# A written-out instruction order exchanged for another one, with one output store moved to a second queue

## Chip, cores and metric

The kernel runs on one core of one Trainium2 chip, as one launch. The metric is the device time of the launch in microseconds (us); shorter is better. Before the change it took 362.02 us (median of 3 runs, 361.42 to 363.49).

## What is computed

The inputs go through a linear attention with a decaying state, then a gated two-layer block. With batch B=4, heads H=8, sequence S=768, head size D=48, and x of width 384 made of the heads' outputs:

```python
for t in range(S):                                   # attention
    cur = einsum('bhd,bhe->bhde', u * k_t, v_t)
    y[:, :, t] = einsum('bhd,bhde->bhe', r_t, state + cur)
    state = w_t[..., None] * state + einsum('bhd,bhe->bhde', k_t, v_t)
h = gelu(x @ w_in)                                   # 384 -> 1024, tanh form
u, v = h[..., :512], h[..., 512:]
v_n = (v - mean(v)) / sqrt(var(v) + 1e-6) * g_ln
v_s = einsum('ts,bsd->btd', w_sg, v_n) + b_sg        # over the sequence
out = x + (u * v_s) @ w_out                          # 512 -> 384
```

## The kernel before, in words

The recurrence is done in 24 chunks of 128 time steps, six to a batch. A chunk's decays are running products over time (`decays`, lines 562 to 585, VectorE scans), its keys and receptances are scaled by them, and the rest of a chunk is small matmuls. The gated block works per batch on 128 rows for v (`v_piece`, L954) and on halves of 384 columns for u, the gate and the output (`u_piece`, `gate_piece`, `out_piece`). Each product of it is three matmuls with the operands split in a high and a low part (L950, L951, L952). The last batch's gate uses sums of halves of the matrices instead (`first_sum`, `second_sum`, `third_sum`). Checks of the inputs' range (`range_check`, `f64_check`) run on ScalarE from data loaded for that alone, and end in one flag (`verdict`, L1260) on which the program branches at its end (L1431, L1433).

Nothing is scheduled at run time. Every unit of work is a generator that yields steps, and the string `ORDER` (L40) says in which order the steps are taken and on which engine each one runs: 1785 words such as `p14S`. The first letter is the kind of work, the number its index (chunk or piece), the last letter the engine: P TensorE, D VectorE, A ScalarE, G GpSimd, S SyncE. `run` (L252) goes through the words and `step` (L259) emits each one's instructions, so the words of one engine, from left to right, are that engine's program. Each engine takes its own instructions strictly in this order and waits at one until its inputs, and the buffer that it takes, are there.

Kinds that are spoken of: r, o, q, p are the loads of a chunk's decays, keys and receptances, values, and token-major keys (`load_w` L528, `load_kr` L535, `load_v` L544, `load_rk` L552); w `own_weights` (L622); e `decayed_k`; f `decays`; t `move` (L912), three pairs of small DMAs that put a chunk's outputs in place; C `split_x` (L924), which waits for them; i `f64_check`, y `range_check`, g `early_sums`, n `late_sums`, each a load and then work on it; K `v_piece`, J `u_piece`, m `gate_piece`, u `out_piece`, M `verdict`. A word of J, m or u on TensorE is three matmuls.

E is `stretch` (L819), one word on TensorE for chunks 6 to 23. It takes together the last products of chunk n, products of chunk n+1 and scores of chunk n+2. Between its first group of matmuls (`pe_own`, L701) and a later group that uses the array's rows in another way, `behind` (L664) puts an instruction of SyncE:

```python
fence = nc.sync.nop()                                   # L667
tc.add_manual_dep(fence.ins, first.ins.name, sync, reason="row tiles")
tc.add_manual_dep(then.ins, fence.ins.name, sync, reason="row tiles")
```

SyncE waits there for the first group and TensorE's later group waits for SyncE. There are 18 of these marks, one in each stretch. SyncE also issues every DMA of the kernel, so a DMA whose word stands behind an E word is issued after that stretch has begun, however early its buffer is free.

TensorE's results go to four accumulators of one bank each (`m_ps`, three of them, and `resets` after chunk 7), which ScalarE or VectorE must empty before TensorE can use them again.

Of the kernel before, what the change touches and what calls it, by code (L numbers as in the profile page):

```python
# [45 lines left out]
c0S o4S p4S t1S t1S t1S q3S q5S v2P z3P f4D s3D e4G k4D f4D h0A w4D h0D w4D j3A C0A K0P K0P F2A F2A H3A j4A d3A K0P
K0A K0G p5S r5S C1A j5A C1G a4A k3P H4P k3A x3P w4D D3D f4D f5D H4A q4S h1S t2S t2S o5S t2S v3P D3D f5D f5D k5P w5G
w5G w5D K1P v3A v3P x4P w4A K1P K1P h5S h4S h3S d4A f4G D4D f5D D4D e5G z4P o7S r6S o6S p6S p7S F3A F3D h1A C2A f5D
h1D k5A f5G s4D K1A K1D C2D h4A h4D H5P H5A a5A h3A h3D h5A h5D k4P k4D v4P x5P K2P J1P K2P K2P d5G v4A v4P K1A K1D
K1G K0A K0G D5D w5A f6D f6D F4A F4A z5P K1G K0G w6D w6G K0G J3P J3P J1P s5D f6D e6D K1A K1A K1D w7D v5P v5A J1P J1A  # L50
# [10 lines left out]
u0P w10G m7D f11D f11D r12S p13S o12S e11G t6S t6S t6S I10A m7A s10D m7D w11D w11A D9D D9D u0D w13G w13G m6P m6P m6P
m5P m6P m6D m6D f12D d10A r13S m6A m6D e12D f12D C6G C6D p12S m5P m5P m5P E9P w12D m5P m4P m4P m4P K6P K6P f13D I11A
C7A C7D F9A w12G D10D D10D F9D s11D o13S q11S u0S q12S f12D f12D K6P C8A K6A K6D K6A C8G r14S m5P m5D w12D f13D e13D
w12D w13D K7P m4P K7P K7P K7A K7D E10P K8P f13D f13D d11A F10A K6D K6G w13G I12A K7A F10A D11D s12D m5D m5A f14D m4P
# [2 lines left out]
t7S t7S t7S o15S q13S r15S C9A C9G s13D K8A K6D K8D w15D D12D w14D u3P u3P J9P J9P K8A K8D K8G C10A u5D w15D r16S u4S
J9P J9A w14A u5S K9P K9P K9P u3P K8D K8D f15D C10D K8A K8D K9A C11A K9G K9A C11G J8P E12P s14D J8P J8P K9G K9G K9G u3P
f16D u3D p16S p17S u3S o17S f15D f15D K11P w15A I14A K11P K11P K11A K11D d13G K9A K9G a16A K11A J8A F12D D13D D13D K9D
f15D F12A e15D K10P K10P K10P K10A K10G J13P J13P m9P w16D w16G a15G w16D f16D J13P J13A m10P m10P m10P E13P m11P m11P  # L70
# [5 lines left out]
m13P m13P o18S C12A C12G d16A E15P w19D D16D w19D w19D f19D C13A C13G a19G D16D o19S J15P J15P J15P J15A m12P m12P
m12P m14P m13P s17D f18D f19D e18D f19D f19D m13D m13D w18A I17A F15A F15A q18S p20S r20S d17A C14A e19G w20G C14G
w20G m12P m12P m15P m15P m12D m12D m13A m13D m12A m12D E16P f20D D17D f20D s18D w20D F16A F16D r21S o20S m14P m14P
m15P m15P m15P K12P K12P K12P K12A K13P m15P K13P K13P K12D e20D I18A K12A K12D f20D m14P m14P m14P m14D w19A K13A
E17P K12G a20G K13G f21D f20D K13A K13D m14D s19D w20A F17D F17D f21D K12G K12G a21G K12G D18D D18D I19A K13G K13D  # L80
# [5 lines left out]
J23P J23P J19P J23P J21P K17P J19A J21P J21P J21A I21A K17P K17P K17A K17D J23A J17P J17P F19A J17P J17A i6S i6A K17A
K17D K17G K17G m16P w23D w23D f23D f23D f23D K17A K17A K17D q22S p22S o22S q21S m18P J22P f22D D20D m17P m17P m17P
m17P m18P m16P m16P m16P m16P J22P J22P m18P m18P m17P m18P m16P m16D m16D m16A e22G d21A m17P m17D m18P m16D w23A
J22A E20P w22G w22G a22G w22D w22D m18D m18D D21D D21D m19P I22D m17D s22D m18A F20A F20A m17A m18D m17D m19P m19P
# [275 lines left out]
def rwkv_gmlp(ctx: ExitStack, tc: tile.TileContext, wpad, kr, vtok, ktok, vt, u, ucol, w_in, consts_, w_sgT, w_out, out):  # L365
    nc = tc.nc
# [1244 lines left out]
```

## Time and profile before

| | before |
|---|---|
| median of 3 runs | 362.02 us (361.42 to 363.49) |
| the profiled execution | 365.26 us |
| its span, first to last instruction | 363.5 us |
| mean granted TensorE clock | 0.986 |
| busy: TensorE, VectorE, ScalarE, GpSimd | 343.0, 273.3, 222.1, 139.2 us |
| DMA: packets' share of the 16 engines' span | 49.9% |

The span is what the trace covers; 1.8 us of the profiled execution lie outside it. Busy time of an engine is the time in which it had an instruction of its own running; waits, branches and DMA issues are not counted. Every number of the trace comes from that one execution.

### The profile page before, as it was taken

What the parts mean: (1) busy time and instruction counts of PE and PEld (TensorE: products, weight loads), DVE (VectorE), ACT (ScalarE), POOL (GpSimd) and SP (SyncE); (2) the same over time, 40 slices, a digit from 0 to 9 for tenths busy, and PEclk for the clock granted to TensorE, in tenths of its full rate; (3) what the DMA queues carried; (4) which work ended last, traced back from release to release, by engine and by line L of the source; (5) the groups of instructions that cost most, each with busy time, mean ns of one, the idle gap of its engine ahead of it and who ended that gap; (6) DMA issues with size and microseconds to landing.
All of it is one profiled execution on the core that took longest, in us unless ns stands there. A gap on an engine that the chain in (4) does not pass through costs nothing.

```text
span 363.5 us, 11014 instructions
## 1 busy us (share of the span) xinstructions
PE 343.0 (94%) x4447; PEld 314.9 (87%) x4447; DVE 273.3 (75%) x537; ACT 222.1 (61%) x598; POOL 139.2 (38%) x222
## 2 busy tenths in 40 slices
PE   7997999999999996999999998999979869999995
PEld 6785788899999895899999897889977869999994
DVE  7998899998998839867779795756734234777684
ACT  1776997886445535862626663483443397898782
POOL 8283641217343223365415233633021836126500
PEclk9899999999999998999999999999999989999999
DMA  7978994512385274424266117431254765534542
GB/s 261 350 266 274 310 338 146 201 59 91 128 261 173 71 245 122 166 89 140 64 206 189 45 34 261 133 130 60 70 153 146 246 213 180 156 128 125 182 151 91
DMA packets 28470, 60.46 MB, mean 166 GB/s; under 512 B 3456, under 2 KB 13184, under 8 KB 28416
## 3 DMA queue, kind: packets, MB, share of 16 engines
q1 hardware_dynamic: 28416, 59.73, 49.9%
q8 instruction: 36, 0.59, 0.6%
q14 instruction: 18, 0.15, 0.1%
HBM read 53.82 MB, written 4.72 MB: 161 GB/s over the span
## 4 chain that ended last, share of the span: by engine, by line
PE 73%; DMA 8%; POOL 5%; ACT 5%; DVE 4%; issue 3%; SPq 1%; POOLq 0%; DVEq 0%
PE m_ps L950 14%; PE m_ps L952 13%; PE m_ps L951 13%; PE resets L950 4%; PE a_ps L678 4%; PE resets L951 4%; PE resets L952 4%; PE y_ps L701 3%; PE y_ps L712 2%; DMA vtok<-in_w_sgT 2%; DMA KR<-in_wpad 2%; DMA RK<-in_ktok 2%; DMA x<-y 1%; PE y_ps L685 1%; PE m_ps L481 1%
## 5 line engine op out<-in xcount | busy, mean ns | idle before, releaser
L950 PE MATMUL m_ps<-wsgh,vn 128*128 128x384 f32 x114 | 39.6, 347 | 2.0 <-DVE o L1256 2.0
L653 ACT ACTIVATE a<-KR,own 128x64 f32<-128x64 f32 x152 | 38.3, 337 | 5.1 <-DVE own L647 4.1
L952 PE MATMUL m_ps<-wsgh,vn 128*128 128x384 f32 x114 | 38.7, 340 | 0.0
L951 PE MATMUL m_ps<-wsgl,vn 128*128 128x384 f32 x114 | 38.7, 340 | 0.0
L950 PE MATMUL m_ps<-xT,winh 128*128 128x384 f32 x87 | 30.8, 354 | 3.2 <-DVE o L1256 2.9
L952 PE MATMUL m_ps<-xT,winl 128*128 128x384 f32 x87 | 29.7, 341 | 0.0
L951 PE MATMUL m_ps<-xT,winh 128*128 128x384 f32 x87 | 29.7, 341 | 0.0
L617 POOL TENSOR_TENSOR KR<-KR,W 128x512 f32<-128x512 f32 x14 | 16.7, 1190 | 23.5 <-DVE KR L585 13.0
L987 POOL TENSOR_TENSOR st<-st,mhalf 128x1 f32<-128x1 f32 x24 | 13.8, 575 | 29.1 <-DVE st L985 13.4
L950 PEld LDWEIGHTS m_ps<-wsgh,vn 128*128 128x128 f32 x114 | 21.9, 192 | 3.1 <-DVE o L1256 2.3
L950 PE MATMUL m_ps<-g,wouth 128*128 128x384 f32 x72 | 24.3, 337 | 0.0
L952 PE MATMUL m_ps<-g,woutl 128*128 128x384 f32 x72 | 24.2, 336 | 0.0
L951 PE MATMUL m_ps<-g,wouth 128*128 128x384 f32 x72 | 24.2, 336 | 0.0
L678 PE MATMUL a_ps<-KR 64*64 64x128 f32 (+1 forms) x768 | 22.8, 256 | 0.0
L1016 ACT ACTIVATE u<-m_ps 128x384 f32<-128x384 f32 x29 | 14.1, 487 | 13.3 <-PE m_ps L952 13.2
L951 PEld LDWEIGHTS m_ps<-wsgl,vn 128*128 128x128 f32 x114 | 21.9, 192 | 0.3
L701 PE MATMUL y_ps<-a,vtok 64*64 64x64 f32 x768 | 21.4, 224 | 0.8 <-ACT a L979 0.8
L701 PEld LDWEIGHTS y_ps<-a,vtok 64*64 64x64 f32 x768 | 16.2, 134 | 6.6 <-issue 2.5
L952 PEld LDWEIGHTS m_ps<-wsgh,vn 128*128 128x128 f32 x114 | 21.7, 191 | 0.0
L950 PE MATMUL m_ps<-winh,xT 128*128 128x512 f32 x45 | 18.6, 414 | 3.2 <-DVE g L1052 3.2
L372 ACT COPY x<-y_ps 128x384 f32<-128x384 f32 x20 | 9.6, 478 | 19.3 <-PE y_ps L701 7.3
L568 DVE TENSOR_TENSOR_SCAN W<-W,D 128x516 f32<-128x516 f32 x16 | 21.0, 1315 | 0.2 <-DMA W<-in_wpad 0.2
(372 smaller groups left out, 1085.7 us busy)
## 6 DMA issues: line engine op xcount, KB each, us to landing
KR<-in_kr SPq DMA_DIRECT2D x24, 512.0 KB, 4.9
RK<-in_ktok SPq DMA_DIRECT2D x20, 384.0 KB, 4.2
W<-in_wpad SPq DMA_DIRECT2D x24, 258.5 KB, 3.3
KR<-in_wpad SPq DMA_DIRECT2D x9, 517.0 KB, 3.8
vtok<-in_vtok SPq DMA_DIRECT2D x24, 192.0 KB, 4.5
out<-o SPq DMA_DIRECT2D x21, 192.0 KB, 3.0
vn<-in_w_in SPq DMA_DIRECT2D x6, 512.0 KB, 6.1
KR<-in_w_in SPq DMA_DIRECT2D x6, 512.0 KB, 4.1
```

The source lines that it names most:

```text
L372: nc.scalar.copy(o, i) if e == "ACT" else engine[e].tensor_copy(o, i)
L568: nc.vector.tensor_tensor_scan(Suf[:, WL - 1:0:-1], W[:, WL - 1:0:-1], r_one if early else D1[:, WL - 1:0:-1], 0.0, ALU.mult, ALU.add)
L617: engine[op.e].tensor_tensor(cols(x.K), cols(x.K), blocks(x.Suf, 2), ALU.mult)
L653: nc.scalar.activation(a[:, j, p], eyes, AF.Copy, scale=o[:, j, p:p + 1])
L678: nc.tensor.matmul(ps_[64 * c_:64 * c_ + 64, j, p * C:p * C + (2 * T if c_ < turn else T)], x.K[rows, at:at + T], r_, start=True, stop=True)
L701: m = nc.tensor.matmul(place(y, j, q, r, c_), x.V[64 * c_:64 * c_ + 64, h * D - up(p, j):h * D - up(p, j) + 64], x.a.tile[64 * c_:64 * c_ ...
L712: m = behind(m, nc.tensor.matmul(place(y, j, q, r, c_), S2.tile[64 * j:64 * j + 64, 16 + 64 * p - up(p, j):80 + 64 * p - up(p, j)], x.R[64 ...
L950: nc.tensor.matmul(ps, lh, rh, start=(i == 0), stop=False)
L951: nc.tensor.matmul(ps, lh, rl, start=False, stop=False)
L952: nc.tensor.matmul(ps, ll, rh, start=False, stop=(i == n - 1))
L987: nc.gpsimd.tensor_tensor(rstd, var, c.mhalf, ALU.pow)
L1016: nc.scalar.activation(h_.u[f].tile, ps, AF.Gelu_apprx_tanh)
```

## The change

The 1785 steps are the same, with the same arithmetic, and `ORDER` takes them in another order. 207 of them run on another engine: 59 go from GpSimd to VectorE and 58 the other way, 26 each way between GpSimd and ScalarE, 20 from ScalarE to VectorE and 17 back, one from SyncE to ScalarE. The 515 TensorE words are the same 515 in another order. An output store of the last batch may now name ScalarE, whose own DMA queue it then uses; one word does, `u23A`, the last half of the last piece. The rest of the file is unchanged.

The diff, cut to the stretches that are spoken of below:

```diff
 ORDER = """
-r0S o0S b0S r1S w0G w0P w0A f0D f0D f0D f0D f0D e0G f0G f1D f1D f1D k1S k1D f1D k1D o1S H0P z0P w0A w1D w1P j1A k1D
...
-m4D J11P J11P J11P J11A K8P E11P m4D m4A m5D m4D F11A F11A p15S u2S p14S o14S J10P J10P J10P J10A u4P I13A q14S a13G
-K7G K7G w14G w14D K7G f14D K6D u5P u5P u5P u5P u4P u4P u4P K8P K7D w15D e14D f14D f14G K7A D12D u4D K7D K6A K6A a14G
...
-K13D q19S J18P J18P J18P J18A u11P E18P u11P I20A o21S u8S t9S r23S p23S t9S t9S q20S o23S u11P u10P u11P u9P u9P J19P
...
-m19P J20P J20P J20P J20A m19P m19P m19D m19D m19A E21P I23D d22G i1S i1A g0S g0S g0G g0G m19D g0D g0D y1S t10S t10S
-t10S y1S q23S C18A C18G D22D D22D y1A y1A u12P u13P u13P u13P u12P u14P u14P u13P m20P m20P u13D u13S s23D m20P m20P
...
-C19D g1S g1S g1D g1G g1G F22A F22D D23D K18P K18P K18P K18A K18G C20G C20G K18A K18D K18G K18G K18G K18G g1G K18G K18G
-E23P m22P m22P F23D F23D m21P m22P m22P m21P y4S y4A y4A u14S i8S y2S y2S i8A m22D m22D m22A m22D K20P m23P i5S i5A
...
-y11A M0D M0D M0D M0D u22P u23P u21P u23P u22P u21P u21P u23P u23D u23S M0D u23D u23S M0D u21P u21D u21S u22P u22P
-M0D u22D u22S M0P M0D
+r0S o0S w0G f0D f0D f0D f0D f0D e0D r1S b0S f0G f1D k1S k1D k1D w0P w0A w0A a1A j1A o1S q0S k2S r2S H0P z0P w1G w1P
...
+D8D D8D w10A a10G u0D m7P m7P m7P m4P p11S o11S f11D f11D f11D f11D m7P m7P m7P m7D E8P F8A m4P F8D w11D w11D p12S u1S
+r12S q10S u2P u2P w11D u2D e11G d9G m4P w12G w12G m4P m4P m4P m5P m5P m5P m5P m6P m5P m6P I10A q11S t6S t6S t6S m7D
...
+w12A a13G C8G C8G w13D K6G w13D f13D f13D K7P E10P J11P K7P d11G K6A K7A K7G K7A J11P J11P J8P J8P K8P K8P K8P J11A
+F10D F10D D11D s12D m5D m5D K6G K6G K6G e13G f14D K7D q15S p14S o14S I12A E11P J8P r15S o15S K6A K6A K6D m5A m5D K7G
+K7G K8A w13D w13D f14D F11A F11A a14A J8A I13A K8G K8A t7S t7S q13S t7S J9P u5P J9P J10P J10P J10P J10A J9P w14D f14D
...
+o18S f18D u8P u8P u8P u8D w20D E15P D16D f18D D16D f18D r19S t8S t8S q17S t8S u8S o19S u6P f18D u6D u7P u7P C12A C12D
...
+w19G w19D w19A f20D K13P K13P K13P E17P f21D K13A K13D m13D F17A F17D s19D o21S p21S e20G f20D t9S q21S t9S t9S K13A
...
+m16P e22D f22G m18P m16P m16P m18P m17P m16P m16D m16D m16A d21A m16D w23G w23G m17P m17D m17D m17A m19P E20P f23D
+F20A F20A w22D w22G D21D D21D I22A w23D w23G J20P J20P J20P J20A m19P s22D m19P m19D m17D m19D u11S i8S i8A t10S t10S
+t10S C18A C18G J21P J21P m18P m18P m18P J21P J21A m19A m18P m18D m18D m18A m18D i5S i5A d22G C19G C19D u12P u12P E21P
+m19D u14P u14P u14P g1S g1S g1G g1G i9S i9A q23S I23D u12P u12P u12D u12S i2S i2A u13P u13P u13P u13P m22P m22P g1D
...
+K19G K19G E23P F23A F23A i1S i7S t11S t11S t11S m21P y3A y3A m23P m23P m23P m23D m23D m23A m21P m21P m21P m21D m21D
...
+u23P u22P u21P u22P u19S u18D u18S u23P u21P u21P u22P u23P u21P u21D u21S u22P u22D u22S u23P u23D u23S u23D u23A M0D
+M0D M0D M0D M0D M0D M0D M0P M0D
 """
...
     def dma(kb, **kw):
-        return Op({"SP": 0.62 if kb in (16, 48) else 0.47}, kb=kb, **kw)
+        return Op(kw.pop("on", {"SP": 0.62 if kb in (16, 48) else 0.47}), kb=kb, **kw)
...
-            yield dma(192 // parts, free=[o], apart=k < parts - 1)
-            nc.sync.dma_start(out[b, ms, half * HALF + k * w:half * HALF + (k + 1) * w], o.tile[:, 0:w])
+            op = yield dma(192 // parts, free=[o], apart=k < parts - 1, **({"on": {"SP": 0.47, "ACT": 0.47}} if b == B - 1 else {}))
+            (nc.scalar if op.e == "ACT" else nc.sync).dma_start(out[b, ms, half * HALF + k * w:half * HALF + (k + 1) * w], o.tile[:, 0:w])
```

## Rows read from the trace of the kernel before

**Rows 1.** The page's busy times, share of the span and instructions of each engine.
```profile
PE 343.0 (94%) x4447; PEld 314.9 (87%) x4447; DVE 273.3 (75%) x537; ACT 222.1 (61%) x598; POOL 139.2 (38%) x222
```

**Rows 2.** Waits of TensorE: for whom; us in total, times, longest.
```profile
PE m_ps L950 <- DVE o L1256: 4.9, 2, 2.9
PE m_ps L950 <- DVE g L1052: 3.2, 1, 3.2
...
PE resets L950 <- ACT xT L372: 0.9, 1, 0.9
PE y_ps L701 <- ACT a L979: 0.8, 1, 0.8
...
PE resets L952 <- POOL xT L945: 0.4, 1, 0.4
```

**Rows 3.** Windows: length; busy PE, PEld, DVE, ACT, POOL; PEclk; DMA share, GB/s.
```profile
0.00:10.00 10.00, 7.54 (x40) 7.07 (x41) 7.60 (x15) 2.58 (x7) 8.75 (x35) 0.92 0.79 261
...
70.00:80.00 10.00, 10.00 (x113) 9.10 (x112) 9.96 (x25) 8.32 (x23) 1.55 (x4) 1.00 0.09 30
...
140.00:150.00 10.00, 9.17 (x139) 8.31 (x140) 9.96 (x20) 6.79 (x22) 4.00 (x6) 0.83 0.34 105
...
290.00:300.00 10.00, 6.82 (x25) 5.71 (x24) 3.11 (x6) 9.46 (x23) 3.81 (x8) 0.83 0.63 211
```

**Rows 4.** Waits of SyncE's queue: the 18 marks of the stretches.
```profile
SPq L667 <- PE y_ps L701: 89.3, 18, 9.3
```

**Rows 5.** Timeline of SyncE, 100 to 145 us: start, us, then the issue.
```profile
120.40 0.33 SPq L533 DMA_DIRECT2D W<-in_wpad  x1
128.43 0.33 SPq L556 DMA_DIRECT2D RK<-in_ktok  x1
...
129.29 0.42 SPq L556 DMA_DIRECT2D RK<-in_ktok  x1
```

**Rows 6.** Timeline of TensorE, 126 to 148 us.
```profile
127.77 0.46 PE L701 MATMUL y_ps<-a,vtok 64*64 64x64 f32 x16
...
130.20 0.44 PE L950 MATMUL m_ps<-xT,winh 128*128 128x384 f32 x1
...
131.35 0.34 PE L950 MATMUL m_ps<-xT,winh 128*128 128x384 f32 x1
...
131.87 0.34 PE L950 MATMUL m_ps<-g,wouth 128*128 128x384 f32 x1
...
140.83 0.44 PE L950 MATMUL m_ps<-xT,winh 128*128 128x384 f32 x1 [2.90 <-DVE o L1256]
```

**Rows 7.** The chain that ended last, in order of time: start, us, what.
```profile
129.29 5.96 DMA RK<-in_ktok
...
219.80 5.05 DMA x<-y
...
261.34 6.55 DMA vtok<-in_w_sgT
...
282.67 6.16 DMA KR<-in_wpad
```

**Rows 8.** Timeline of VectorE, 0 to 20 us: one line of the kernel twice.
```profile
8.91 1.19 DVE L1303 TENSOR_SCALAR vn<-vn 128x512 int32<-128x512 int32 x1
...
13.50 0.41 DVE L1303 TENSOR_SCALAR vn<-vn 128x512 int32<-128x512 int32 x1
```

**Rows 9.** Timeline of all engines from 345 us to the end: the flag's steps.
```profile
356.51 0.17 DVE L1263 TENSOR_SCALAR chk<-chk 128x12 f32<-128x12 f32 x1
...
356.71 0.17 DVE L1265 TENSOR_REDUCE cnt<-chk 128x1 f32<-128x12 f32 x1
...
358.82 0.15 DVE L1275 TENSOR_TENSOR cnt<-cnt 128x1 f32<-128x1 f32 x1
...
359.12 0.19 PE L1278 MATMUL m_ps<-cnt,ones 128*1 128x1 f32 x2
...
359.70 0.14 DVE L1280 TENSOR_SCALAR bad<-m_ps 1x1 int32<-1x1 f32 x1
```

More of the change, by code (lines that the diff above doesn't have):

```diff
@@ L46 @@
[L46 to L50, printed above, removed]
@@ L61 @@
[L61 to L64, printed above, removed]
-m4D J11P J11P J11P J11A K8P E11P m4D m4A m5D m4D F11A F11A p15S u2S p14S o14S J10P J10P J10P J10A u4P I13A q14S a13G
@@ L66 @@
-K7G K7G w14G w14D K7G f14D K6D u5P u5P u5P u5P u4P u4P u4P K8P K7D w15D e14D f14D f14G K7A D12D u4D K7D K6A K6A a14G
[L67 to L70, printed above, removed]
@@ L76 @@
[L76 to L80, printed above, removed]
@@ L86 @@
[L86 to L89, printed above, removed]
-m19P J20P J20P J20P J20A m19P m19P m19D m19D m19A E21P I23D d22G i1S i1A g0S g0S g0G g0G m19D g0D g0D y1S t10S t10S
@@ new lines @@
+w1A H0A w1A f1D f1D f1D k1D k1D k1P s0D f1D e1G k2D f1D k2D k0S k0D k2D k0D v0P H1P z1P s1D k0D x0P k2D k0D f2D f2D
+f2D o3S j2A j0A v0A D0A D0D H1A v0P F0A a2A F0A k1A o2S q3S k0P k0A d1A w2G w2P w2A w2A w3G e2G f2D f2D r3S f2G f3D
+f3D f3D k4S q1S k4D v1P v1A x1P D1D f3D D1D f3D e3G k4D k4D k3S k3D q2S o4S t0S t0S t0S k2P k2A H2P a3A H2A d2A j4A
+v1P z2P w3P F1A F1A C0A k4D k4P k3D f3G h2S h2A h2G s2D w3D r4S x2P f4D k5S c0S D2D D2D f4D w3A f4D f4D v2P v2A p4S
+C0P d3A z3P v2P e4G C0A s3D k5D k3D F2A F2A k4A k5D h0S t1S t1S t1S p5S k3D w4D k5D r5S C1A C1D w4D w5D H3P H3A h0A
@@ new lines @@
+j3A h0G j5A a4A K0P K0P K0P K0A H4P v3P v3A x3P w5G D3D w4D H4A w4A h1S q4S o5S h1A k3P f5D f4D D3D t2S h5S t2S t2S
+K1P K1P v3P x4P f5D k5D K0D d4D f4D e5G D4D D4D f5D a5A k3A C2A C2D h1D F3A h5A F3A k5P h5D k5A h3S h3A h3G K0A K0G
+K1P K1A o6S h4S h4A q5S z4P q6S p6S J1P H5P J1P H5A J1P f5D s4D v4P v4A f5D w5D w5A r6S t3S k6S o8S t3S t3S J2P J2P
+J2P x5P v4P K1D K1A h4D d5D f5D D5D z5P f6D s5D f6D K0G w6G J0P J0P J0P K1G F4A F4A v5P J2A K0G K0A K1G K2P e6D J0A
+k6D w6D k6D K1D k6D v5A v5P K0A C3A C3D j6A k6D K0D k6D k8S k8D o7S r7S F5A F5A t4S t4S t4S p8S k6D k8D J1A K1A K1A
@@ new lines @@
+K1D k8D f7D H6P H6A t5S t5S t5S C4A C4G K2P K2P j8A K2A K2D k8D e7D k8D K3P K3P K3P K3A K3D K2A K2D k8D C5A C5G J3P
+J3P J3P J3A K3A a7G K3G K2G K4P x6P H7P H7A q8S D6A f6D w6D w6A K3G K2G K3G K3A K2A f6D f6D f6G K4P K4P D6D f7D f7D
+f7D f7D k9S k9D f7D k9D k9D k7S q7S k9D K2A K2D w8D J4P J7P J7P J4P J4P J4A k7D k7D J7P J7A K3A K4A K4D K4A K3D j7A
+k7D k7D K4D k7D p7S r9S r8S z6P s6D K4G J6P J6P J6P m1P j9A w7D K5P K5P K5P K5A K5D K5A m1P m1P m1P m0P K4D K4A k9D
+k7D k9D m0P m0P m0P z7P J6A K5D w8D w7D w8D w7D K5G K5G K4A K4D f8D K5A K5A K5D m2P m3P m3P m2P m2P f8D f8D f8G w7G
@@ new lines @@
+m0P m3P m3P m0P m0D m0D m0A e8G m1P m1P m1D a8A m0D m1D m1A s7D p10S o9S p9S r10S f9D w8A m2P m2P m2P m2D m3P m3P J5P
+d7A J5P J5P J5A m1D m2D m2A m3D m3D m3A a9A m2D f9D E6P w9G e9G w10G m3D f9D f9G u0P u1P u0P u1P u2P u1P u2P u1P u0P
+u0P o10S r11S q9S F6A I8A D7D F6A s8D D7D E7P w9D w9D w9A d8A F7A I9A F7A w10D w10D f10D e10G u1D f10D f10D f10G s9D
+D8D D8D w10A a10G u0D m7P m7P m7P m4P p11S o11S f11D f11D f11D f11D m7P m7P m7P m7D E8P F8A m4P F8D w11D w11D p12S u1S
+r12S q10S u2P u2P w11D u2D e11G d9G m4P w12G w12G m4P m4P m4P m5P m5P m5P m5P m6P m5P m6P I10A q11S t6S t6S t6S m7D
@@ new lines @@
+K7D K7A f14D w14D s13D w14D K8G K8G K8D f15D f15D J9A K7D C9A C9D e14D C10G C10G e15G u4P K8A K8A u3P u3P u3P p16S
+p15S u4P u4P u4P u4D u5P u5P u5P u3P r16S u5D u5S C11A D12A D12D K8D C11D w15D w15D K9P K9P K9P K9A K9D d13A E12P f15D
+K9A K9G K9G I14A K9G w14A D13D f15D D13D q14S a15G K9A K9A u3D F12D w16D f16D s14D J15P J15P K11P K11P K11P J15P K11A
+K11G F12A K11A K9D m9P K10P K10P K11D K11G w16D K10P K10A J15A r17S K10G m10P E13P K11D K11G K11G w15D w16D d14A K10A
+K10G K10G F13D F13A K10D f16D m10P m10P K11G m9P m9P m10P m8P w15D K10A K10A K10D a16G o17S o16S p18S u4S p17S q16S
@@ new lines @@
+u3S f16D m8P m8P m8P m8P m8P m8D m8D I15A D14D D14D f17D m8A m8D s15D e16G f16G m9P m11P m11P m9P m9P m9D m9D m9A m9D
+e17G f17D m11P m10P m10P m11P m11P m10D m10D m10A m10D J12P m11P m11D d15A E14P J14P J14P m11D F14D F14A u6P u6P u6P
+J14P J14A w18G w16G w18G w18D f17D f17G s16D m11A m11D J12P J12P J12A u8P D15D D15D w17D I16A a17A w17D d16D r18S p20S
+o18S f18D u8P u8P u8P u8D w20D E15P D16D f18D D16D f18D r19S t8S t8S q17S t8S u8S o19S u6P f18D u6D u7P u7P C12A C12D
+C13G J13P m15P u7P u7P J13P m15P q18S u7D u7S u6S f19D w17D I17A F15A F15A J13P J13A d17G e18G w17D m15P m15P m15P
@@ new lines @@
+m12P m12P m15P s17D m15D r20S p19S m13P m14P m12P m12P m12P E16P m13P w18A F16A e19G C13G f19D f19D f19D I18A m15D
+m15A m15D w20G D17D m13P m13P m13P C14G C14G a19A r21S o20S q19S F16D w20D w19G s18D f20D f20D m13P m13D m13D m13A
+w19G w19D w19A f20D K13P K13P K13P E17P f21D K13A K13D m13D F17A F17D s19D o21S p21S e20G f20D t9S q21S t9S t9S K13A
+K13G K13G K13G m14P m14P m14P m14P m14P m14D m14D K12P K12P K12P K12A K12G K12A K12G K12G m12P D18D m12D m12D I19D
+D18D K13A K13A w21D K13D m14A m14D m12A e21G m12D K14P C15A a21A C15D K14P K14P K14A K14G a20A J18P J18P J18P E18P
@@ new lines @@
+K14A J18A I20D w21D w21D K14G K14G K14D K12D K12A K12A u11P f21D f21D K14G w20G q20S r22S p23S p22S d19A f21G J17P
+u10P u10P u11P u10P u10P u10D u10S o23S K14A K14D r23S u9P u9P u9P K15P K15P u9P u9D u9S s20D C16A C16D K15P K15A u11P
+J17P u11P u11D J17P D19D F18D F18D D19D K16P J19P K16P K15G K15A K15G K15G K15D K15D K15A f23D E19P e23D C17A K15D
+C17D f22D K16P J19P K16A J17A K16G K16A a22A K12G K16G K16G w21D s21D K16D F19D w22D F19D J23P J23P J19P J19A K17P
+K17P K17P K17A K17G i3S i3A d20D D20D K17A K17D D20D K17G K17D J22P J22P J22P J22A I21A a23A J23P J23A J16P J16P o22S
@@ new lines @@
+g1G g2S g2S y3S D22D D22D u13D m22P m22P m22P m22P m22D m22D m22A m21P u14P u14D m23P m23P m23P m20P F21D d23D F21D
+m21P C20A E22P s23D m22D D23D F22D F22A g2G C20G g2G g2D g2G K19P K19P K19P K19A K19G K19A K19G K19G K19G K19G K19G
+K19G K19G E23P F23A F23A i1S i7S t11S t11S t11S m21P y3A y3A m23P m23P m23P m23D m23D m23A m21P m21P m21P m21D m21D
+m21A m21D m20P m20P i7A m20P m20P m20P m20D m20D m20A m20D g1G g1G C21A C21D K18P K18P K18P K18A K18D m23D C22G C22D
+K18A K18D K18G g2A C23G C23D K18D K20P K20P K21P K21P i1A K20P K20A K20G y0S y1S g0S g0S g0D g2D K18A K22P K20A K20D
@@ new lines @@
+K20G K22P K22P K22A K22D g0A g0D K20D K22A K22D K22G K21P u17P K21A K21D u16P u17P u17P K23P u17P K23P K20A K21A u14S
+K22G g0D g0G g0D K20D K22A K22G K18G K21G K21G y0S y0A y0A K20A y1S y1A y1A n0S u13S n2S n2S K23P u17D u17S J27P u16P
+u16P u16P u16D u16S J27P J27P J27A L1D K21D L1D L1G n2D J29P J29P J29P J29A K21A L1D L1G u15P u15P K22D L1D L1D y11S
+n0S u15P u15P u15D K20D L1A L1D J26P J26P J26P n1S n1S K18A K18D n2D K23A K23D J26A K23A y11A J28P J28P J24P J24P J25P
+J25P y11A J28P J28A l1P J24P l1P J24A y2S y2S y2A J25P J25A y2A G1P l0P l0P l0P L0G L0D n2G K23G K23G n1D L0G K21G
@@ new lines @@
+K23G L0G G0P G0P G0P n1D K21D n0D n0D n0D n1D B0P l1P l1D n0G K23A l0A K23A K23D B0P G1P l0P n1A n1D y5S n2A L2D n0G
+L2G y5A i0S i0A y5A l0P l0P G0D l0D l0D G1P G1D l1P l1P l1P l1D l1D n2G L0G L0G L0D L2A l0A l0D L2G l1A l1D n2A n2G
+G0P G0P G1P G1P G0P G1P B0P B0D n1G n0A n0D L2G n1G L2G L2G L2G L2G y9S y9A y9A u15S L0G L0G u20P B1P B1P G0D u18P G0D
+G0D G0A B1P B1D B0P B0P u20P B0P G0D G1D B1P u19P u19P u20P u18P u18P i4S i4A y8S y8A y8A G1D B0D B0P B0P G1D G1A G1D
+B0P B0D B0D B0D B1P B1P u19P y6S y6A y6A y4S y4A B0A y4A B1D u20P u19P u19D u18P B0D u20D y10S y10A y10A B1P B1P B1P
@@ L110 @@
+y7S J30P J30P J30P J30A B1D B1D B1D B1A J31P J31P J31P J31A A0D A0D A0A i6S u20S i6A B1D A1D A0D A1D A1A A1D y7A y7A
+u23P u22P u21P u22P u19S u18D u18S u23P u21P u21P u22P u23P u21P u21D u21S u22P u22D u22S u23P u23D u23S u23D u23A M0D
+M0D M0D M0D M0D M0D M0D M0P M0D
 """
```

41 lines of the change are left out of this document (3 added, 38 removed).

## The prediction

> **What bounds the kernel now.** I read the busy shares first. TensorE is busy 343.0 of 363.5 us, VectorE 75%, the others less [rows 1]: TensorE is the engine that sets the time, and since the change keeps its 515 words, it can only take away what TensorE waits or what makes it slow. Then the waits of TensorE, without the first 45 us: 4.9 us in two waits for an output piece's add (2.9 and 2.0), 3.2 us in one wait for a gate piece, and 0.9, 0.8 and 0.4 us behind ScalarE and GpSimd [rows 2]. That is 10.2 us. The windows add what a wait leaves behind. In the stretches that hold the 2.9 us and the 3.2 us wait the granted clock is 0.83 where it is 1.00 elsewhere [rows 3]: part of the stretch runs at 1.2 GHz instead of 2.4, and 0.17 of 10 us, 1.7 us, are lost in each. The 2.0 us wait left no such dip. So the stalls cost 10.2 + 3.4 = **13.6 us**.
>
> Who makes TensorE wait is not the engine that the wait names. The chain of waits leads, a little ahead of each of the four places, to a DMA: 5.96 us for a chunk's token-major keys, 5.05 us for a move, 6.55 us for rows of w_sg, 6.16 us for a range check's data [rows 7]. Their landing times are ordinary; they were issued late. SyncE's timeline shows it for the first: an issue at 120.40, nothing for 8 us, then at 128.43 and 129.29 the two loads of keys [rows 5]. In between, SyncE stood at the mark of stretch 11, whose first group started on TensorE at 127.77 [rows 6]. SyncE's waits sum this up: 18 marks, 89.3 us, up to 9.3 each [rows 4]. A load behind a mark is late; the engine that first needs it stands still, in order, with all that is queued behind; the banks fill; TensorE stops at 137.9 and goes on at 140.83 [rows 6].
>
> **The change part by part.** *The loads behind marks.* I measure each load by the TensorE time between the E word ahead of it in the order and the first word that uses it. A stretch is 130.20 - 127.77 = 2.4 us, and a word of three matmuls 131.87 - 131.35 = 0.52 us [rows 6]. In the old order `p14S` stands behind `E11P`, and up to its user `w14G` TensorE has the stretch, three J10P and one u4P: 2.4 + 4 x 0.52 = 4.5 us. It needs from stretch 11's start at 127.77 until the issue at 129.29 and the landing at 129.29 + 5.96 = 135.25: 7.5 us [rows 6, 7]. It is 3 us short, and GpSimd stands for that time with the keys' first product, VectorE behind it with the second.
>
> Going through both orders in this way (values aside, which are loaded far ahead): in the old one 15 loads have under 6 us, behind seven marks: 8 (4.0), 11 (4.5), 18 (5.9), 19 (3.8), 21 (2.4), 22 (2.1), 23 (4.6). The stalls follow them at all but mark 8. In the new order seven loads have under 6 us, behind four marks: 8 (p12, 4.5), 15 (move 8, 4.0), 20 (move 10 and a check, 5.0), 21 (g1, i9, 4.0; i2, 5.0). `p14S` now stands ahead of E11P, behind E10P, 14 us ahead of `w14D`; move 9 is behind E17P with 8 us and not behind E18P; and where five late loads stood behind E23P, only i7 and i1 and move 11 do, with 6 us or more. Every place that cost TensorE a stall in the old order has been taken apart.
>
> What do the four remaining ones cost? Below, nothing; above, as much per mark as the seven did: 13.6 / 7 = 1.9 each, 7.8 in all. What is queued behind the late user decides. At mark 8 GpSimd's next words belong 5 us later; at mark 21 ScalarE's next is the cast of gate piece 22, more than 5 us later. At mark 15 ScalarE holds a copy and a `taken` behind `C12A`, at mark 20 the gelu `J21A` and a gate's cast, 3 us behind; with four banks TensorE has some words of room. I let mark 20 and part of mark 15 pay: 2.5 us.
>
> *The marks as TensorE's own wait.* If SyncE is held at an issue when a stretch comes, TensorE waits for the mark. The trace shows no such wait that matters, and the same marks remain; I take zero. If a buffer frees late ahead of a mark it would cost that lateness, up to the 1.9 a mark above.
>
> *Steps on another engine.* 59 go from GpSimd to VectorE, 58 back, so the totals stay. From 70 to 80 us VectorE is busy 9.96 of 10 [rows 3]: over the first 80 us it has no spare time, and the same word costs more or less there. In the new order VectorE has 12 more words from GpSimd ahead of TensorE's 65th us and 8 fewer. Adding up its words with their durations in this trace, its work is 2.5 us less ahead of TensorE's 40th us and 3.8 us more ahead of its 70th, so the start can lose 3.8. It can gain no more than TensorE's idle part of the first 10 us, 10 - 7.54 = 2.5 us [rows 3], where `e0D` now runs on VectorE. I take zero between these ends.
>
> One line shows what such moves can do: VectorE's L1303 took 1.19 us at 8.91 and 0.41 at 13.50 [rows 8], 0.78 us more beside a GpSimd instruction. The Trainium skill, "SBUF — State Buffer", section "Who interferes with whom", says that VectorE and GpSimd share a pair of ports, and that of two instructions that need it the later one is blocked until the first is over. By the row alone a moved step costs its own duration and the sum is unchanged; by the rule it may also hold its neighbour, a result of its own that stands among the rivals.
>
> *The flag.* In the old order the verdict's steps lie between the last output pieces, and its last one starts at 359.70, beside the last add. In the new order seven small VectorE steps, a TensorE step and a last VectorE step stand behind the last add. Two that depend on each other start 356.71 - 356.51 = 0.20 us apart, and from the seventh to TensorE 359.12 - 358.82 = 0.30 pass; then 0.19 and 0.14 [rows 9]. At most 6 x 0.20 + 0.30 + 0.19 + 0.14 = 1.8 us come behind the add; the steps that do not depend on each other go faster, and the last stores land beside them. Between 0 and 1.8 I take 1.1 us, lost.
>
> *The store on ScalarE's queue* (`u23A`) can save one issue of SyncE, 0.42 [rows 5], at a time when the flag is late anyway: zero. A second queue has no row here; I bound it by one issue either way.
>
> **The sum**: 13.6 - 2.5 - 1.1 = 10.0 us less. The profiled execution took 365.26, span 363.5, and would take 355.3; it lies 3.2 us above the median of the runs, so the median of 362.02 becomes **352.0 us**. Its own ends: no remaining stall, a flag at no cost and 2.5 us won at the start give 345.9; 7.8 for the marks, 1.8 for the flag 358.0.
>
> **The rivals.** *Four marks pay in full.* The four short marks cost what a mark did on average, 7.8 us, and the flag 1.1: 362.0 - 13.6 + 7.8 + 1.1 = 357.3. For it: the leads of 4 to 5 us are all under the 7.5 that the load behind mark 11 needed. Against it: what is queued behind the users.
>
> *VectorE is held in the start.* Eight steps come to GpSimd from VectorE ahead of TensorE's 65th us. If each holds a VectorE instruction by 0.78 us as in [rows 8], and VectorE has no spare time there [rows 3], the start loses 6.2: 358.2. It is the case that the skill's rule on the ports speaks for. Against it: VectorE gets rid of work with each of these steps, and the order places GpSimd's steps by VectorE's.
>
> *The marks matter, the leads do not.* Taking 7.5 us as the need, nine marks have a load that is short in the old order, and nine in the new. If the number of such marks sets the loss, 13.6 comes back and the flag is added: 363.1, no change to speak of. The change would then not do what its layout says. Against it: the stalls of the old order follow the shortest leads.
>
> *Slower: four stalls with the clock.* Both waits of 2.9 us and more brought the clock down, so one of them costs 2.9 + 1.7 = 4.6. If marks 8, 15, 20 and 21 each make such a wait, 18.4 + 1.1 us come for 13.6: 362.0 + 5.9 = 367.9. It decides from (13.6 - 1.1 + 1.8) / 4 = 3.6 us a mark. Four loads are 2.5 to 3.5 us short of 7.5, as the one behind mark 11 was, which speaks for it; that only the queues behind the users can turn this into a TensorE wait speaks against.
>
> **How the numbers follow.** A difference of 0.5%, 1.8 us, is about what the measurement can tell from none. I give the forecast 0.63, the four marks in full 0.15, VectorE in the start 0.07, no change 0.07, slower 0.08. Faster by over 0.5% are the first three, 0.85; same 0.07; slower 0.08. The range goes from 346.5 to 358.5: it takes in the forecast's own ends and the first two rivals, and leaves out the last two (0.15) and a little below.
>
> **What would show it.** In the new trace: no TensorE wait of 2 us or more behind marks 11, 18, 21 to 23; both dips of the clock in mid-kernel gone; the loads behind the marks landed ahead of their users, so that GpSimd's and ScalarE's long waits for DMAs of w_sg rows and checks are gone; a tail of VectorE steps behind the last add about 1 us longer. A wait of over 2 us near stretches 8, 15, 20 or 21, a new dip of the clock, or TensorE reaching stretch 6 later than before would speak for a rival. A time above 360 would prove the reading by leads wrong.

## The result and the profile after

The changed kernel takes **348.11 us** (median of 4 runs, 347.97 to 350.20) where the kernel before took 362.38 beside it (361.42 to 363.49): ratio 0.961, 95% interval 0.957 to 0.966. Predicted were 352.0, between 346.5 and 358.5. The execution that the profile shows took 350.20, span 348.4, against 365.26 before: 15.06 us less, and that difference is taken apart below.

The page of the changed kernel first, its busy times [rows 1] and the chain that ended last:

```profile
PE 340.0 (98%) x4453; PEld 313.9 (90%) x4453; DVE 273.0 (78%) x541; ACT 213.5 (61%) x564; POOL 148.2 (43%) x221
...
PE 91%; ACT 3%; POOL 2%; DMA 2%; DVE 1%; issue 0%; SPq 0%; POOLq 0%; ACTq 0%
```

TensorE is busy 98% of the span. Its waits [rows 2], for whom, us in total, times, longest:

```profile
PE m_ps L1278 <- DVE cnt L1275: 1.6, 1, 1.6
PE m_ps L481 <- POOL junk L458: 1.3, 1, 1.3
PE m_ps L481 <- POOL same L468: 0.6, 1, 0.6
PE m_ps L634 <- POOL RK L629: 0.5, 1, 0.5
PE a_ps L685 <- ACT kt L372: 0.4, 1, 0.4
PE m_ps L950 <- ACT look L372: 0.3, 1, 0.3
```

All of these lie in the first 45 us or, the first row, behind the last product. The waits for output pieces (L1256) and gate pieces (L1052) have no row any more. The windows [rows 3], with one of the start added:

```profile
10.00:20.00 10.00, 10.00 (x123) 8.60 (x123) 7.83 (x17) 5.29 (x20) 2.48 (x2) 0.76 0.87 303
...
140.00:150.00 10.00, 10.00 (x152) 8.90 (x151) 8.29 (x17) 6.21 (x20) 3.46 (x6) 1.00 0.22 71
...
290.00:300.00 10.00, 10.00 (x57) 9.64 (x56) 5.81 (x15) 9.22 (x16) 4.15 (x8) 1.00 0.54 185
```

In mid-kernel TensorE is busy 10.00 of 10 where it was 9.17 and 6.82, at a granted clock of 1.00 where that was 0.83. SyncE, on the other hand, is still held at its marks for 75.8 us, where it was 89.3 [rows 4]:

```profile
SPq L667 <- PE y_ps L701: 75.8, 18, 10.3
```

What differs is what stands in front of a mark. SyncE's timeline around mark 11 [rows 5]; stretch 11 starts on TensorE at 129.08 here, 127.77 before:

```profile
124.08 0.38 SPq L556 DMA_DIRECT2D RK<-in_ktok  x1
124.51 0.42 SPq L542 DMA_DIRECT2D KR<-in_kr  x1
129.73 0.33 SPq L533 DMA_DIRECT2D W<-in_wpad  x1
```

The load of chunk 14's keys is issued 5.0 us ahead of the stretch's start instead of 1.5 behind it. Last, the end of the timeline [rows 9]:

```profile
342.58 1.15 DVE L1256 TENSOR_TENSOR u<-m_ps,x 128x384 f32<-128x384 f32 x3
...
343.64 0.16 DVE L1263 TENSOR_SCALAR chk<-chk 128x12 f32<-128x12 f32 x1
...
344.69 0.19 PE L1278 MATMUL m_ps<-cnt,ones 128*1 128x1 f32 x2 [1.62 <-DVE cnt L1275]
344.91 0.15 DVE L1280 TENSOR_SCALAR bad<-m_ps 1x1 int32<-1x1 f32 x1 [0.28 <-PE m_ps L1278]
```

The verdict's steps begin behind the last add and end 1.3 us after it. From the end of the last product (L952) to the end of the span pass 5.32 us, 4.35 before.

**Where 15.06 us came from.** I took the start of each stretch and of the groups between, subtracted TensorE's own work up to there, and compared the two traces. What is left is time lost. Between 138 and 147 us of the old trace 4.8 us go, at 224 to 228 1.8, at 238 0.5, at 270 2.2, at 276 to 283 1.2, and at 290 to 299 5.0: 15.5. The start gains 0.4, although it holds 6.8 us at half clock in this execution and 3.4 in the one of before, a loss of 1.7 us more. The tail loses 0.97. Sum: -15.5 - 0.4 + 0.97 = -14.93.

### The profile page after: what moved, and what is told of

Same layout as the page of the kernel before. It is cut to its first block, busy times and chain, and to the rows that moved or that the text cites. A ratio compares the mean times of both kernels' runs of the same rounds, so it can differ in the third digit from the quotient of the medians.

```text
span 348.4 us, 10988 instructions
## 1 busy us (share of the span) xinstructions
PE 340.0 (98%) x4453; PEld 313.9 (90%) x4453; DVE 273.0 (78%) x541; ACT 213.5 (61%) x564; POOL 148.2 (43%) x221
## 4 chain that ended last, share of the span: by engine, by line
PE 91%; ACT 3%; POOL 2%; DMA 2%; DVE 1%; issue 0%; SPq 0%; POOLq 0%; ACTq 0%
PE m_ps L950 17%; PE m_ps L952 16%; PE m_ps L951 16%; PE resets L950 6%; PE resets L951 6%; PE resets L952 6%; PE a_ps L678 5%; PE y_ps L701 4%; PE y_ps L712 3%; PE y_ps L685 2%; DMA x<-y 2%; PE m_ps L481 2%; PE m_ps L1145 1%; PE a_ps L1145 1%; PE m_ps L724 1%; PE y_ps L1145 1%
## 5 line engine op out<-in xcount | busy, mean ns | idle before, releaser
L950 PE MATMUL m_ps<-wsgh,vn 128*128 128x384 f32 x114 | 39.1, 343 | 0.0
L952 PE MATMUL m_ps<-wsgh,vn 128*128 128x384 f32 x114 | 38.4, 337 | 0.0
L653 ACT ACTIVATE a<-KR,own 128x64 f32<-128x64 f32 x120 | 30.4, 342 | 4.1 <-DVE own L647 4.0
L617 POOL TENSOR_TENSOR KR<-KR,W 128x512 f32<-128x512 f32 x18 | 21.8, 1216 | 23.6 <-DVE W L568 8.1
L950 PE MATMUL m_ps<-g,wouth 128*128 128x384 f32 x80 | 27.3, 341 | 0.0
L952 PE MATMUL m_ps<-g,woutl 128*128 128x384 f32 x80 | 26.9, 336 | 0.0
L951 PE MATMUL m_ps<-g,wouth 128*128 128x384 f32 x80 | 26.9, 336 | 0.0
L1050 ACT CAST g<-m_ps 128x384 fp32r<-128x384 f32 x21 | 9.9, 477 | 27.0 <-DVE m_ps L1048 27.0
L950 PE MATMUL m_ps<-xT,winh 128*128 128x384 f32 x75 | 25.9, 345 | 0.0
L952 PE MATMUL m_ps<-xT,winl 128*128 128x384 f32 x75 | 25.2, 336 | 0.0
L951 PE MATMUL m_ps<-xT,winh 128*128 128x384 f32 x75 | 25.2, 336 | 0.0
L987 POOL TENSOR_TENSOR st<-st,mhalf 128x1 f32<-128x1 f32 x24 | 14.7, 613 | 20.2 <-DVE g L1322 6.3
L1046 DVE SCALAR_TENSOR_TENSOR m_ps<-m_ps,flat 128x384 f32<-128x384 f32 x21 | 13.0, 618 | 12.1 <-PE m_ps L952 11.3
L952 PEld LDWEIGHTS m_ps<-wsgh,vn 128*128 128x128 f32 x114 | 21.4, 188 | 0.3 <-DVE vn L1002 0.3
L585 POOL TENSOR_TENSOR KR<-KR,W 128x512 f32<-128x512 f32 x12 | 14.8, 1231 | 14.3 <-PE m_ps L952 3.7
```

Source lines behind the costliest of these rows:

```text
L585: engine[op.e].tensor_tensor(cols(x.R), cols(x.R), blocks(W, 0), ALU.mult)
L617: engine[op.e].tensor_tensor(cols(x.K), cols(x.K), blocks(x.Suf, 2), ALU.mult)
L653: nc.scalar.activation(a[:, j, p], eyes, AF.Copy, scale=o[:, j, p:p + 1])
L950: nc.tensor.matmul(ps, lh, rh, start=(i == 0), stop=False)
L951: nc.tensor.matmul(ps, lh, rl, start=False, stop=False)
L952: nc.tensor.matmul(ps, ll, rh, start=False, stop=(i == n - 1))
```

## The experiments

**The marks kept, the loads moved.** The old order with 19 SyncE words, loads and moves, ahead of the mark that they stood behind (the expectation below counts them as 18); nothing else changes. Its core, three of the places, the lines shortened at both ends:

```diff
-K8P E11P m4D m4A m5D m4D F11A F11A p15S u2S p14S o14S
+K8P p14S E11P m4D m4A m5D m4D F11A F11A p15S u2S o14S
-J18A u11P E18P u11P I20A o21S u8S t9S r23S p23S t9S t9S
+J18A u11P o21S t9S r23S t9S t9S E18P u11P I20A u8S p23S
...
-E23P m22P m22P F23D F23D m21P m22P m22P m21P y4S y4A y4A u14S i8S y2S y2S
+y4S i8S y2S y2S E23P m22P m22P F23D F23D m21P m22P m22P m21P y4A y4A u14S
```

> The old order with 18 SyncE words alone moved: the loads that stood close behind the marks of stretches 11, 18, 19, 21, 22 and 23 (one keys load, a move and three other loads, the sums' rows, two checks) are put directly ahead of these marks; three whose buffer is not free there stay. Words of the other engines are untouched, engines too. Theory (loads queued behind SyncE's marks make the stalls): TensorE's waits after 45 us fall from 10.2 us to under 4, both half-clock stretches in mid-kernel go, the time falls by 9 to 13 us to 349 to 353. Rival 1 (the new places and engines of the other words carry the gain): 358 to 363. Rival 2 (SyncE, held at these loads ahead of a mark, now holds TensorE at the mark): no faster than 361, with waits of TensorE for the mark's line.

Measured: 351.05 us (349.40 to 352.16), ratio 0.966 (0.962 to 0.970), 13.0 less than the kernel before, run beside it (364.00). TensorE's waits:

```profile
PE m_ps L481 <- POOL junk L458: 1.3, 1, 1.3
PE a_ps L685 <- ACT kt L372: 0.8, 1, 0.8
...
PE m_ps L950 <- ACT u L1016: 0.4, 1, 0.4
...
PE y_ps L712 <- SPq L667: 0.2, 1, 0.2
```

The longest wait from 45 us on is 0.8 us, at 46 us; the long stalls are gone with all 18 marks and all old engines in place. So the loads' places behind marks were the cause, and they carry most of the gain.

**The stalls one by one.** Two parts of the same edit: first `p14S` alone, the first pair of diff lines above; then only the twelve words ahead of marks 21, 22 and 23.

> The kernel before with one word moved: the load of the keys of chunk 14, p14S, from four SyncE words behind mark 11 to directly ahead of E11P. My theory (each stall is the work of its own late loads, and the stalls add up): the wait of 2.9 us at 141 and the half clock behind it go, 4.8 us by the difference of the two traces there, and the other stalls stay: 4.8 less than the kernel before in the same call, 358.9 where that is 363.7. Rival (the engines run late by then, and the next late load takes the stall over): less than 2 us, with a new wait of over 2 us between 141 and 240.

> The kernel before with twelve SyncE words moved ahead of marks 21, 22 and 23 (i1, two g0, three t10; two g1; y4, i8, two y2), the others left. My theory: the stalls from 270 us on go, 2.2 + 1.2 + 5.0 = 8.4 us by the difference of the two traces, those at 141, 227 and 238 stay: 8.4 less than the kernel before in the same call, 355.3 where that is 363.7; with the one load at mark 11 that makes 13.2 of the 13 to 14 that all eighteen words brought. Rival (the late engines carry lateness from mark 18 to the later marks): under 5 us, and a wait of 2 us or more behind 265 us.

Measured: one word gives 360.39 (358.68 to 364.02), ratio 0.992 (0.989 to 0.996); twelve give 354.88 (354.05 to 358.33), ratio 0.980 (0.974 to 0.985); before, beside them, 363.98. By the medians 3.6 and 9.1 us, 12.7 together, where all 19 words brought 13.0; by the ratios 2.9 and 7.5, 10.4 together, where all brought 12.4. So the stalls add up to within some 2 us, which is also what the six words left out, at marks 18 and 19, can be worth. The rival that lateness is handed on fell: the first kernel has no wait of over 1 us between 141 and 240. The 3.6 is short of the 4.8 expected. With TensorE's words the same in both, stretch 11 to stretch 12 takes 15.55 us in the first kernel's trace and 19.51 in the one before, 4.0 less; the 4.8 came from the new order, whose other words differ. Here are the waits that stay, in the first kernel and then the second, each with its window:

```profile
PE m_ps L950 <- DVE g L1052: 3.0, 1, 3.0
...
280.00:290.00 10.00, 7.05 (x37) 6.20 (x36) 3.01 (x6) 5.84 (x13) 5.46 (x9) 1.00 0.83 295
```

```profile
PE m_ps L950 <- DVE o L1256: 2.8, 1, 2.8
...
130.00:140.00 10.00, 7.22 (x41) 6.78 (x40) 5.45 (x11) 3.42 (x7) 2.51 (x4) 1.00 0.62 224
```

Waits as long as those of [rows 2] stand here at a clock of 1.00, in these stretches and the next ones. A half-clock stretch behind such a wait comes in some traces and not in others; 1.7 us is what it cost where it came.

**A load made late, in two doses.** In the changed kernel, three loads for chunk 14 are moved from ahead of mark 11 to directly behind it, and then to directly ahead of their first user (`w14D`, chunk 14's first `own_weights` step on VectorE). The first edit, cut to the words around the mark:

```diff
-K7D q15S p14S o14S I12A E11P J8P r15S o15S
+K7D I12A E11P q15S p14S o14S J8P r15S o15S
```

> The new order with three SyncE words put back behind the mark of stretch 11, where the old order had two of them: q15, p14 and o14 directly behind E11 instead of ahead of it. In the new kernel VectorE reached the user of p14 2.7 us after stretch 11's start, so it would stand there until the load lands, some 7 us after that start: 4 us. Theory (a load late at its engine stops TensorE once the queue behind is needed): one TensorE wait of 1 to 4 us near 135 to 142, and where it reaches some 3 us a half-clock stretch of 1.7 us more; time 349 to 354. Rival by the leads alone (6.6 us in the order, 0.9 short): no change, 348.0 within 0.7. Rival that the place of these loads does not matter at all: no change and no wait of VectorE either.

> The same three loads still later, directly ahead of the first word that uses one (p14's, on VectorE), behind the three DMAs of a move. In the new kernel the move was issued at 134.7, so the keys would land near 141 and VectorE stand 9 us. Theory: TensorE stops for 5 to 8 us, with a half-clock stretch; time 354 to 359. Rival (TensorE has work enough in its own order to cover it): under 350.

Measured: 349.19 (348.53 to 350.13) for the first and 354.45 (353.94 to 354.73) for the second. The first is a miss of my theory: about 1 us, and no wait of TensorE of 1 us or more. Its rows on VectorE, GpSimd and TensorE:

```profile
125.48 1.69 DVE L568 TENSOR_TENSOR_SCAN W<-W,D 128x516 f32<-128x516 f32 x1
...
132.48 0.56 DVE L642 TENSOR_TENSOR RK<-RK,flat 128x384 f32<-128x384 f32 x1 [2.92 <-DMA RK<-in_ktok]
...
136.80 1.23 DVE L568 TENSOR_TENSOR_SCAN W<-W,D 128x516 f32<-128x516 f32 x1
...
124.89 1.20 POOL L617 TENSOR_TENSOR KR<-KR,W 128x512 f32<-128x512 f32 x1
...
PE resets L950 <- ACT xT L372: 0.2, 1, 0.2
```

VectorE stands 2.92 us for the keys, and TensorE waits 0.2. From stretch 11 to stretch 13 TensorE takes 24.69 us, against 23.71 in the changed kernel: the load costs some 1.0 us in all, of which the view of waits shows 0.2. In the second kernel VectorE stands 6.81 for the same keys and, three steps on, 1.0 for a second load; now TensorE waits and the clock falls:

```profile
136.70 0.56 DVE L642 TENSOR_TENSOR RK<-RK,flat 128x384 f32<-128x384 f32 x1 [6.81 <-DMA RK<-in_ktok]
...
144.66 0.67 PE L952 MATMUL resets<-winh,xT 128*128 128x512 f32 x1 [3.60 <-DVE xT L945]
...
140.00:150.00 10.00, 6.06 (x117) 4.51 (x121) 9.93 (x19) 3.94 (x11) 3.87 (x5) 0.83 0.24 87
```

7.8 us of VectorE's waiting cost TensorE 0.6 + 3.6 = 4.2 in waits, less than the 5 to 8 expected: by this estimate VectorE had about 3.6 us in hand there.

**Order and engines taken apart.** The new order with each moved step on its old engine, and the old order with each on its new one (207 of 1785 words differ, as in `K6G` for `K6D`).

> The new order, but each of the steps that the change moved to another engine runs on its old one; the outputs' queues as in the change. My theory: the gain is the loads' places, the engine moves cost and bring nothing (the step of the prediction that was priced at 0): about 348.1, within 1 us, with no TensorE wait of 1 us or more after the first 20 us. Rival: the old order with the loads ahead came to 351.05, 2.9 us above the changed kernel, and that remainder is the engines': then this kernel gives about 351, with VectorE or GpSimd named in TensorE's waits of the first 80 us. Third: an order written for other engines does worse than both, over 352, with new waits of TensorE wherever a moved step stands behind a long one.

> The old order, but each moved step runs on its new engine. My theory: the four late places of loads stay, so about 362.4, within 2 us, and the TensorE waits of 2.9, 2.0 and 3.2 us near 138, 290 and 147 us are still there with the dips of the clock behind the longer ones. Rival (the engines carry the remaining 2.9 us of the gain): about 359.5, with the three long waits still there. Third: over 364, because steps stand behind others that the old order had not put on their engine.

Measured: 394.76 (392.73 to 395.71) and 393.65 (392.71 to 397.60): some 46 us slower than the changed kernel, 30 slower than the kernel before. The third expectation held in both, far beyond its size. TensorE waits all through the kernel in the first, and its clock falls to half in five places from 25 us on up to the last product (the page's row of 40 slices):

```profile
PE m_ps L950 <- DVE g L1052: 3.2, 2, 2.8
PE y_ps L701 <- DVE S L779: 3.1, 3, 1.2
...
PEclk9598999999999989999999999999899899998999
...
POOL st L987 <- DVE st L985: 25.4, 10, 5.2
```

and in the second:

```profile
PE y_ps L701 <- DVE S L771: 5.1, 1, 5.1
PE y_ps L701 <- DVE y L372: 3.5, 1, 3.5
...
PEclk9999999999899999999999999699999699999999
```

`POOL st` shows one way in which it can come about. The small steps of a normalisation are passed from engine to engine; where one is put on an engine for which the order did not plan, it stands behind that engine's other words, and the next engine waits: GpSimd 25.4 us in ten waits, 6.0 in five in the changed kernel. How much of the 46 us goes this way was not measured. These two runs give no price for the engine moves alone; they show that this order and its engines can't be exchanged one by one.

**The tail.** Four kernels, all the changed one but for its last words. First the verdict early: six VectorE steps ahead of the first add, the seventh behind the second, TensorE's step behind the last product. Second the one store of ScalarE's queue back on SyncE's. Third and fourth the early verdict with the last products in another sequence (piece 23 first; piece 22 first). The core of the first, the lines shortened at the front:

```diff
-u23P u21P u21D u21S u22P u22D u22S u23P u23D u23S u23D u23A M0D M0D M0D M0D M0D M0D M0D M0P M0D
+u23P u21P M0D M0D M0D M0D M0D M0D u21D u21S u22P u22D M0D u22S u23P M0P u23D u23S u23D u23A M0D
```

> The new order with the verdict's steps moved alone: six of the seven small VectorE steps ahead of the last three output adds, where VectorE stands idle, the seventh behind the second of them, TensorE's step behind its last product. Theory (the flag's chain is what ends last): the end comes 0.9 to 1.2 us sooner after the last product, TensorE's 1.6 us wait for the flag goes, time 347.0 within 0.5. Rival (the last store's landing ends the kernel anyway): under 0.3 us of difference.

> The changed kernel with its one store on ScalarE's queue back on SyncE's. My theory: 348.1, within 0.4: the flag is issued later than this store in the changed kernel, so one issue of 0.42 us more on SyncE lies ahead of the flag's own and costs between 0 and 0.4. Rival: ScalarE's queue was what kept the tail from growing more: 0.5 us or more slower, 348.6 and above. Rival on the other side: starting a second queue costs more than it saves, and the time falls by 0.3 or more.

> The changed kernel with its last 26 words rearranged: the products of output piece 23 end four words ahead of the last one, those of piece 21 two words ahead; the first six steps of the verdict stand ahead of the first add, the seventh behind the two adds of piece 23, the verdict's product ahead of TensorE's last word and its last step ahead of the last add. My theory: the tail from the last product to the end of the span goes back from 5.3 to the old kernel's 4.35 us, since neither the flag nor the last add is late: 348.1 - 1.0 = 347.1 (0.5 under the version with the flag early, in which the steps pushed the adds back by 0.45). Rival: the last store's landing sets the end however the steps stand: 347.7, the tail at 4.9. A third: TensorE waits for the verdict's sum or for a gate in the new order of the products: a wait of 0.3 us or more on the last words and no gain.

> The changed kernel with its last 26 words rearranged in another way: the products of output piece 22 end four words ahead of the last one, those of 21 two ahead, those of 23 last, so that the two last stores are the half pieces on two queues as in the changed kernel; six steps of the verdict ahead of the first add, the seventh behind it, the verdict's product ahead of TensorE's last word. My theory: the last adds end 0.66 us behind the last product, the flag ahead of them, and the span 4.35 behind it (5.32 in the changed kernel): 1.0 us less than the changed kernel. Rival (what made the last version's last store land 1.7 us later than the old kernel's is an early verdict and not the store's size): the tail stays at 5.3 or more, and the time at the changed kernel's or above.

> The changed kernel itself, beside the next one on the same chip: 348.1, between 347.9 and 350.2 for a single execution, as at first.

Measured: verdict early **347.75** (347.48 to 349.30), store on SyncE 348.50 (347.90 to 350.45), piece 23 first 349.91 (349.20 to 350.79), piece 22 first 349.69 (349.22 to 352.67), the changed kernel beside the last one 348.55 (347.67 to 349.63). With the verdict early the tail is 4.86 us instead of 5.32:

```profile
341.86 0.61 DVE L1256 TENSOR_TENSOR u<-m_ps,x 128x192 f32<-128x192 f32 x2
342.00 0.19 PE L1278 MATMUL m_ps<-cnt,ones 128*1 128x1 f32 x2 [0.62 <-DVE cnt L1275]
342.39 0.14 DVE L1280 TENSOR_SCALAR bad<-m_ps 1x1 int32<-1x1 f32 x1
```

Counted from the last product, the flag is there 0.8 us sooner, but the steps ahead of the first add push the last adds back by 0.45, and half of it is left, 0.46 where 0.9 to 1.2 were expected. It is the fastest version, by less than its runs differ. The store's queue makes no difference, in the time or in the tail (5.31). The last two kernels miss: their tails are 6.06 and 5.55. The flag and the adds are in time, and it is the last store that lands late. The rows of stores with their KB and median time to landing, in the changed kernel and then with piece 22 first:

```profile
out<-u ACTq DMA_DIRECT2D x1, 96.0 KB, 1.9
```

```profile
q8 instruction: 1, 0.02, 1.6%
...
out<-u ACTq DMA_DIRECT2D x1, 96.0 KB, 3.5
```

An instruction packet (the q8 row) stands in the same stretch in the changed kernel too, so it alone doesn't explain the 3.5. Why the store is slow there was not found.

## Why the prediction was right, step by step

- *The stalls of 13.6 us go.* Right in mechanism and place: the old order with its loads ahead of the marks has none of them. The size is 15.5 rather than 13.6: four waits of 0.12 to 0.30 us that I left out are 0.75 of the rest, and the other 1.1 is about what the view of waits leaves out. Matmuls of 0.34 us start 0.17 us apart, and a wait is counted from the end of the one before; so each of the six long waits ahead of such a matmul cost some 0.17 us more than its row says, an estimate of 1.0 in all.
- *2.5 us stay behind four marks.* This is the term that was mis-sized: TensorE has no wait over 0.15 us from 45 us up to the last product. I took the lead, TensorE time up to the first user, as the measure, with 7.5 us as the need. The two doses show what it leaves out: the user itself had some 3.6 us in hand, and a load that was 2.9 us late at its user cost TensorE a wait of 0.2. The changed kernel's own trace says the same at the four marks. ScalarE stands 7.1 us for move 8 behind mark 15, up to 182.45, and GpSimd 4.4 us for rows of w_sg behind mark 21, the first of its two waits below; the late loads behind marks 8 and 20 hold no engine for more than 1.2 us. No wait of TensorE follows any of them:

```profile
ACT xT L372 <- DMA x<-y: 9.1, 3, 7.1
...
POOL vtok L1123 <- DMA vtok<-in_w_sgT: 9.0, 2, 4.6
```

"What is queued behind the late user decides" was the better sentence, and I then gave it too small a weight.
- *Long waits for DMAs gone on GpSimd and ScalarE.* Wrong as a sign: ScalarE still waits 9.1 us for moves and GpSimd 9.0 for rows of w_sg, and TensorE does not wait behind them.
- *Marks as TensorE's own wait: zero.* Right: TensorE waits 0.12 us twice for a mark, though SyncE is held 75.8 us.
- *Engine moves and start: zero.* Right for the start as it was measured, which gained 0.4 with 1.7 us more lost at half clock; that it came out near zero is in part luck of the execution. TensorE reaches stretch 6 at 88.61 us instead of 87.41, a sign that I had given for a rival; but 112 words stand ahead of it instead of 109, 1.6 us of work, and no time is lost. The rest of the change brings a little: the profile of the old order with its loads ahead and the second one of the changed kernel (347.67 us), both with no half clock ahead of the last product, have spans of 347.6 and 346.0, 1.6 us apart. The changed kernel's longer tail hides another 1.0, so the rest of the order and the engine moves together are worth some 2.6 us. Which of that is order and which engines, the swapped kernels can't tell. The row on a moved step's neighbour holds: in the first dose's rows VectorE's scan L568 takes 1.69 us beside GpSimd's L617, which ran 0.61 us into it, and 1.23 later. This agrees with the Trainium skill, "SBUF — State Buffer", "Who interferes with whom", by which the later of two such instructions is blocked by the earlier. The 0.46 us reach no TensorE wait. That VectorE has no spare time in the first 80 us was read too widely off one window: before the change it was busy 7.60 of the first 10 us and 7.88 from 30 to 40. From 10 to 20 us it was busy 9.86, the row below, and is now busy 7.83:

```profile
10.00:20.00 10.00, 9.58 (x120) 6.92 (x118) 9.86 (x21) 6.39 (x21) 3.00 (x3) 0.91 0.99 361
```

- *The flag: 1.1.* Measured 0.97 in the tail.
- *The store on ScalarE's queue: zero.* Right: 348.50 without it, 348.55 and 348.11 with it.

The rivals: four marks in full, and four stalls with the clock, fell with the changed kernel's trace, where no such wait stands, and the first dose shows why; VectorE held in the start fell with TensorE's start, which lost nothing; "the marks matter" fell with the old order's marks kept. Between the two profiled executions the gain is 15.06 where I had 10.0: 2.5 from the residual stalls, 1.9 from the stalls' size, 0.4 from the start, 0.1 from the flag. The medians, 362.02 and 348.11, show 1.15 us less of it, and so the forecast is off by 3.9.

## What to carry to other kernels

A wait in a queue that issues DMAs cost nothing by itself here: SyncE was held 75.8 us and TensorE 0.2 for it. Look for what is issued right behind it, and ask how far ahead of the bounding engine its first user runs. Late by less than that, it costs little: 2.9 us late cost 1.0 in one place here, and one load of the keys, the third DMA behind a mark, cost 3.6 to 4.8 in another. Don't change the engine of steps in an order that was laid out with others: here both halves of that exchange, each without the other, were slower than the kernel before.

## What I had not expected of the hardware

- The clock: waits of 2.9, 3.2 and 3.6 us were followed by half clock, waits of 2.77 and 2.95 us in other runs were not, and in the swapped kernels waits of 1.44 and 2.28 us were. The start has 6.8 us at half clock in one profiled execution of the changed kernel (350.20) and none in the other (347.67); three of its variants have 3.4. The 2.4 us between the spans of the two are there already at stretch 11 (129.08 and 126.66). It is not all of the spread: two executions with a mean granted clock of 0.996 took 347.69 and 349.63.
- The same 96 KB store took 1.9 us to land in one tail and 3.5 in another.
